# First block of a transformer kernel: norms and transposed copies in quarters over four PSUM banks, x tile 2 loaded ahead of the second V weights, and tile 3's norm moved up in the program

The kernel runs on one core of a Trainium2 chip. The metric is its device time in microseconds (us), the median of several runs. Runs of one and the same kernel lie up to 1.8 us apart (696.97 to 698.73).

In what follows TensorE (PE in the profile, PEld for its weight loads) multiplies and transposes, VectorE (DVE) computes norms, ScalarE (ACT) takes square roots and copies results out of PSUM, the memory that TensorE writes into; the Sync queue (SPq) issues transfers (DMA). A line of a profile gives start and length in us, then engine, line of the kernel, operation, what is written and read, and the number of instructions.

## The reference

A block of a transformer on 2048 rows of 1024 columns: layernorm, Q, K and V projections, attention in a window of 256, output projection, residual, then a second layernorm and a SiLU feed-forward layer.

```python
x = A_x
h = x + _A_ref(_layernorm(x, axis=-1), A_wqkv, A_wo)     # _A_ref: x @ wqkv, windowed softmax, @ wo
h2 = h + _B_ref(_layernorm(h, axis=-1), B_w1, B_w2)      # silu(x @ w1) @ w2
```

Only the first 512 rows' layernorm and V projection matter here: four tiles of 128 rows, normed on VectorE, transposed, and multiplied with the V weights in two column halves.

## The kernel before

Loads, in the order of the Sync queue (x tile 1 goes over ScalarE's queue):

```python
    load_x(0, 0)
    load_wqkv(2 * D)              # V weights 1
    load_x(0, 1, nc.scalar)
    load_wqkv(2 * D + 512)        # V weights 2
    load_x(0, 2)
    load_x(0, 3)
    load_wqkv(0)
```

Norm of one tile (statistics and norm on VectorE, square root on ScalarE) and its transposition by TensorE, with the copy out of PSUM on ScalarE:

```python
    def ln_first(xt, st, rs, j, half_done=None, ahead=None):
        ln_stats(xt, st, j, half_done)
        nc.scalar.activation(out=rs[:, j:j + 1], in_=st[:, j, 1:2], func=ACT.Sqrt, bias=eps[:], scale=1.0)
        if ahead is not None:
            ln_half(ahead[0], ahead[1], 0)
        nc.vector.reciprocal(out=rs[:, j:j + 1], in_=rs[:, j:j + 1])
        for h in range(2):
            ln_norm(xt[:, h * 512:(h + 1) * 512], st, rs, j)

    def turn_first(xt, dst, j, halves=(0, 1)):
        for h in halves:
            for i in range(4):
                kt = h * 4 + i
                nc.tensor.transpose(out=tp_ps[h][:, i * P:(i + 1) * P], in_=xt[:, kt * P:(kt + 1) * P], identity=ident[:])
            nc.scalar.copy(out=dst[:, h * 4:(h + 1) * 4, j * P:(j + 1) * P],
                           in_=tp_ps[h][:, 0:512].rearrange("p (k q) -> p k q", q=P))
```

The program order of the first block; each engine takes its own instructions in this order:

```python
    ln_first(x_ring[0], st, rs, 0, None, (x_ring[1], half))
    turn_first(x_ring[0], lnT_b[0], 0)
    ln_first(x_ring[1], st, rs, 1, half)

    def turn_1(kt):
        if kt in (5, 7):
            turn_first(x_ring[1], lnT_b[0], 1, (kt // 2 - 2,))

    v_group(0, 0, 0, act, turn_1)      # block, tile, column half: 8 matmuls and an evacuation on ScalarE
    ln_first(x_ring[2], st, rs, 2)
    v_group(0, 1, 0, act)
    v_group(0, 0, 1, act)
    turn_first(x_ring[2], lnT_b[0], 2)
    ln_first(x_ring[3], st, rs, 3)
    ln_transpose(x_ring[3], lnT_b[0], 3)    # tile 3 is transposed by DMA
    # ... three weight loads (cut)
    v_group(0, 1, 1, act)
    v_group(0, 2, 0, act)
    v_group(0, 2, 1, act)
    nc.scalar.activation(out=dummy[:], in_=eps[:], func=ACT.Exp)
    v_group(0, 3, 0, act)
    v_group(0, 3, 1, act)
```

The softmax here doesn't subtract the row's maximum and nothing guards it: scores larger than these inputs give would overflow.

## Time and profile before

| | before |
|---|---|
| time, median of 3 runs | 697.46 us (696.97 to 698.73) |
| span of the profiled run, mean granted clock | 694.9 us, 1.0 |
| TensorE busy | 684.8 us, 99% |
| landing of x tile 0 | 3.66 us |
| first K or Q matmul (end of the stretch that changes) | 22.59 us |
| from there to the end | 672.36 us |

The span is the sum of a landing (the time at which a transfer's data have all arrived), a stretch of 18.93 us from that landing to the first K or Q matmul, and a remainder in which TensorE stops only at the very end and which the change leaves alone. The measured time is some 2 us longer than the span.

### The profile page before, as it was taken

The page shows a single profiled execution, that of the slowest core. Times are in us where ns is not written, and L with a number is a line of the kernel's source. Part 1 is how long each engine was busy: PE and PEld are TensorE (multiplying, and loading weights), DVE is VectorE, ACT ScalarE, POOL GpSimd, SP SyncE. Part 2 cuts the span into 40 slices and gives each one's busy share as a digit, 9 for nine tenths or more (in the row PEclk, how much of TensorE's full clock was granted, in tenths as well). Part 3 has the DMA queues.
Part 4 walks back from the last instruction along what each step waited for, and adds up shares of the span by engine and source line. Part 5 has one row for each costly group of instructions (what it writes and reads, how often), then busy time and mean ns, then how long its engine had stood idle before and what let it go on. Part 6 is the DMA issues. An engine that isn't in the chain of part 4 may idle for free.

```text
span 694.9 us, 12233 instructions
## 1 busy us (share of the span) xinstructions
PE 684.8 (99%) x5004; PEld 331.4 (48%) x5091; DVE 288.2 (41%) x608; ACT 257.5 (37%) x322; POOL 174.5 (25%) x391
## 2 busy tenths in 40 slices
PE   8999999999999999999999999999999999999998
PEld 3444454555555555544444444444444444444445
DVE  5257646644443448544316134333133251244111
ACT  4326667777777777621310023300033100233000
POOL 1007667777777677500000000000000000000000
PEclk9999999999999999999999999999999999999999
DMA  7742231036240778880023410023300023100010
GB/s 241 257 63 68 41 99 39 18 66 187 70 129 17 211 253 274 190 311 31 31 75 100 107 38 1 1 87 72 83 1 1 10 96 92 45 1 1 30 39 24
DMA packets 76456, 60.83 MB, mean 88 GB/s; under 512 B 50288, under 2 KB 60528, under 8 KB 76400
## 3 DMA queue, kind: packets, MB, share of 16 engines
q1 hardware_dynamic: 76256, 59.78, 29.6%
q8 instruction: 40, 0.66, 0.4%
q10 hardware_dynamic: 144, 0.26, 0.1%
q14 instruction: 16, 0.13, 0.1%
HBM read 39.85 MB, written 8.39 MB: 69 GB/s over the span
## 4 chain that ended last, share of the span: by engine, by line
PE 98%; issue 1%; DVE 0%; DMA 0%; ACT 0%
PE hacc L558 18%; PE hacc L595 17%; PE acc L249 16%; PE acc L595 10%; PE acc L558 9%; PE acc L239 8%; PE acc L268 7%; PE o_ps L340 4%; PE sc L286 3%; PE hacc L268 1%; PE o_ps L355 1%; PE sc L314 1%; DMA r_o<-in_A_x_dram 0%; DVE ln_st L170 0%; PE o_ps L217 0%
## 5 line engine op out<-in xcount | busy, mean ns | idle before, releaser
L331 POOL TENSOR_SCALAR_AFFINE_SELECT r_e<-r_e 128x256 bf16<-128x256 bf16 (+1 forms) x384 | 171.6, 477 | 116.0 <-ACT r_e L323 64.5
L294 ACT ACTIVATE r_e<-sc 128x1024 bf16<-128x1024 f32 x144 | 139.5, 1021 | 45.1 <-PE sc L286 31.0
L595 PEld LDWEIGHTS <-r_a 128*128 128x128 bf16 x952 | 90.8, 98 | 103.0
L558 PEld LDWEIGHTS <-r_w 128*128 128x128 bf16 x896 | 87.3, 98 | 104.8
L595 PE MATMUL hacc<-r_a 128*128 128x512 bf16 (+2 forms) x607 | 122.0, 360 | 0.5
L558 PE MATMUL hacc<-r_e,r_w 128*128 128x512 bf16 x450 | 100.1, 379 | 0.2
L567 ACT ACTIVATE r_n<-hacc 128x512 f32<-128x512 f32 x30 | 17.9, 597 | 178.9 <-PE hacc L558 175.5
L595 PE MATMUL acc<-r_a 128*128 128x512 bf16 x330 | 73.5, 379 | 0.3
L249 PEld LDWEIGHTS <-r_w 128*128 128x128 bf16 x512 | 46.5, 98 | 57.0 <-issue 7.0
L251 DVE CAST r_a<-acc 128x512 bf16<-128x512 f32 x56 | 38.7, 691 | 72.4 <-PE acc L249 55.8
L249 PE MATMUL acc<-r_t,r_w 128*128 128x512 bf16 x241 | 58.5, 380 | 0.8
L249 PE MATMUL acc<-r_w 128*128 128x512 bf16 x245 | 57.6, 380 | 0.6
L268 PE MATMUL acc<-r_o,r_a 128*128 128x512 bf16 x196 | 48.8, 380 | 0.6
L558 PE MATMUL acc<-r_e,r_w 128*128 128x512 bf16 x207 | 48.4, 379 | 0.6
L340 PEld LDWEIGHTS <-r_e 128*128 128x128 bf16 x1152 | 39.5, 96 | 17.0
L323 ACT ACTIVATE r_e<-sc 128x1024 bf16<-128x1024 f32 x36 | 34.9, 1021 | 21.2 <-PE sc L314 20.1
L340 PE MATMUL o_ps<-r_a,r_e 128*128 128x33 bf16 x1152 | 40.2, 178 | 0.0
L610 DVE SCALAR_TENSOR_TENSOR r_t<-hacc,r_t 128x512 bf16<-128x512 f32 (+2 forms) x22 | 14.0, 635 | 56.7 <-PE hacc L595 56.7
L268 PEld LDWEIGHTS <-r_a 128*128 128x128 bf16 x256 | 23.1, 98 | 29.6 <-issue 5.1
L610 DVE SCALAR_TENSOR_TENSOR r_t<-acc,r_t 128x512 bf16<-128x512 f32 x12 | 8.3, 692 | 64.2 <-PE acc L595 58.8
L568 DVE SCALAR_TENSOR_TENSOR r_a<-r_n,hacc 128x512 bf16<-128x512 f32 x30 | 20.6, 688 | 33.0 <-ACT r_n L567 33.0
L558 PE MATMUL hacc<-r_a,r_w 128*128 128x512 bf16 x138 | 32.4, 379 | 0.3
(71 smaller groups left out, 473.4 us busy)
## 6 DMA issues: line engine op xcount, KB each, us to landing
r_w<-in_B_w_dram SPq DMA_DIRECT2D x8, 896.0 KB, 5.1
r_a<-in_B_w_dram SPq DMA_DIRECT2D x7, 1024.0 KB, 7.8
r_w<-in_A_wqkv_dram SPq DMA_DIRECT2D x6, 1024.0 KB, 8.5
h_dram<-r_t SPq DMA_DIRECT2D x16, 256.0 KB, 2.8
r_t<-h_dram SPq DMA_DIRECT2D x16, 256.0 KB, 2.8
out_dram<-r_t SPq DMA_DIRECT2D x31, 128.0 KB, 1.7
r_o<-in_A_x_dram SPq DMA_DIRECT2D x15, 256.0 KB, 4.1
r_e<-h_dram SPq DMA_DIRECT2D x3, 1024.0 KB, 5.6
```

The costliest lines, as they stand in the source:

```text
L239: nc.tensor.matmul(acc, lhsT=lnT_b[b % 2][:, kt, j * P:(j + 1) * P], rhs=wv[:, kt, c * 512:(c + 1) * 512], start=(kt == 0), stop=(kt == KT ...
L249: nc.tensor.matmul(acc, lhsT=wqk[:, kt, col0:col0 + P], rhs=lnT_b[b % 2][:, kt, :], start=(kt == 0), stop=(kt == KT - 1))
L251: copy(out=(qT, kT)[which][b][:, g, :], in_=acc)
L268: nc.tensor.matmul(acc, lhsT=qT[b][:, g, j * P:(j + 1) * P], rhs=wo[:, g, c * 512:(c + 1) * 512], start=(g == 0), stop=(g == G - 1))
L286: nc.tensor.matmul(sc[hh // 2][:, hh % 2, ch * P:(ch + nq) * P], lhsT=kT[t // 4][r0:r0 + DH, g, (t % 4) * P:(t % 4 + 1) * P], rhs=qT[b][r0 ...
L294: nc.scalar.activation(out=e, in_=sc[pair], func=ACT.Exp, scale=scale)
L323: nc.scalar.activation(out=e, in_=sc[pair], func=ACT.Exp, scale=scale)
L331: nc.gpsimd.affine_select(out=ap, in_=ap, pattern=[[0, 2], [0, n], [sgn, P]], compare_op=ALU.is_ge if upper else ALU.is_gt, fill=0.0, base ...
L340: nc.tensor.matmul(o_ps[pair][:, qt * 2 + hh, 0:VW], lhsT=e_of(i, kind, pair)[:, hh, ch * P:(ch + 1) * P], rhs=v[:, b * 4 + kt, g * 4 + pa ...
L558: nc.tensor.matmul(acc, lhsT=w1[:, kt, ft * P:(ft + 1) * P], rhs=ln2T[b][:, kt, :], start=(kt == 0), stop=(kt == KT - 1))
L595: nc.tensor.matmul(acc[:, 0:c1 - c0], lhsT=gT[:, ft, j * P:(j + 1) * P], rhs=w2[ft // 4][:, ft % 4, c0:c1], start=(ft == 0), stop=(ft == F ...
L610: nc.vector.scalar_tensor_tensor(out=t_out[j % 2][:, c0:c1], in0=acc[:, 0:c1 - c0], scalar=0.5, in1=t_in[j % 2][:, c0:c1], op0=ALU.mult, o ...
```

## The change

The intent, as far as the code tells it: norm, transpose and copy tiles in finer pieces, so that the first V matmuls start sooner; give the pieces four PSUM banks of their own (borrowed from the scores, which need them later); and have x tile 2 early enough that tile 3 is ready when TensorE wants it.

```diff
-    ps_sc = tc.tile_pool(name="ps_sc", bufs=1, ...)          # score banks: opened after the first block now
-    sc = [sc_pool.tile([P, 2, 512], F32, name=f"sc{i}") for i in range(2)]
+    ps_tp = tc.tile_pool(name="ps_tp", bufs=1, ...)
+    tp_ps = [tp_pool.tile([P, 1024], BF16, name=f"tp{i}") for i in range(4)]
-    tp_ps = [t[:].rearrange("p a b -> p (a b)").bitcast(BF16) for t in o_ps]
@@ loads
     load_x(0, 1, nc.scalar)
+    load_x(0, 2)
     load_wqkv(2 * D + 512)
-    load_x(0, 2)
     load_x(0, 3)
@@ ln_first
-        for h in range(2):
-            ln_norm(xt[:, h * 512:(h + 1) * 512], st, rs, j)
+        for h in range(4):
+            ln_norm(xt[:, h * 256:(h + 1) * 256], st, rs, j)
@@ turn_first: four pairs of transposes and copies of 128x256 in place of two of 128x512
@@ program order
-        if kt in (5, 7):
-            turn_first(x_ring[1], lnT_b[0], 1, (kt // 2 - 2,))
+        if kt == 7:
+            turn_first(x_ring[1], lnT_b[0], 1)
     v_group(0, 1, 0, act)
-    v_group(0, 0, 1, act)
-    turn_first(x_ring[2], lnT_b[0], 2)
     ln_first(x_ring[3], st, rs, 3)
     ln_transpose(x_ring[3], lnT_b[0], 3)
     # ... three weight loads (cut)
+    v_group(0, 0, 1, act)
+    turn_first(x_ring[2], lnT_b[0], 2)
     v_group(0, 1, 1, act)
```

(The first lines are abridged; warm-up matmuls, which run before the data are there and now write to other banks, are cut.) There are four main parts: quarters, banks, order of loads, and place of tile 3's norm in the program. A fifth goes with the quarters: tile 1's eight transposes now all stand before the last matmul of the first V group (k = 7), where four stood before k = 5 and four before k = 7.

More of the change, by code (lines that the diff above doesn't have):

```diff
@@ L91 @@
     r_n = big.tile([P, 1536], BF16, name="r_n")
-    ps_sc = tc.tile_pool(name="ps_sc", bufs=1, space=bass.MemoryType.PSUM, reuse_waits="tile")
-    sc_pool = ps_sc.__enter__()
-    sc = [sc_pool.tile([P, 2, 512], F32, name=f"sc{i}") for i in range(2)]
+    ps_tp = tc.tile_pool(name="ps_tp", bufs=1, space=bass.MemoryType.PSUM, reuse_waits="tile")
+    tp_pool = ps_tp.__enter__()
+    tp_ps = [tp_pool.tile([P, 1024], BF16, name=f"tp{i}") for i in range(4)]
     o_ps = [ps.tile([P, 8, 64], F32, name=f"o_ps{i}") for i in range(2)]
-    tp_ps = [t[:].rearrange("p a b -> p (a b)").bitcast(BF16) for t in o_ps]
     acc_ps = [ps.tile([P, 512], F32, name=f"acc{i}") for i in range(2)]
@@ L165 @@
     for i in range(11):
-        nc.tensor.matmul(sc[0][:, i % 2, :], lhsT=warm[:, 0, 0:P], rhs=warm[:, 0, :], start=True, stop=True)
+        nc.tensor.matmul(o_ps[i % 2][:].rearrange("p a b -> p (a b)"), lhsT=warm[:, 0, 0:P], rhs=warm[:, 0, :], start=True, stop=True)
     def ln_half(xt, stats, c):
@@ L209, in ln_first, with turn_first @@
         nc.vector.reciprocal(out=rs[:, j:j + 1], in_=rs[:, j:j + 1])
-        for h in range(2):
-            ln_norm(xt[:, h * 512:(h + 1) * 512], st, rs, j)
-    def turn_first(xt, dst, j, halves=(0, 1)):
-        for h in halves:
-            for i in range(4):
-                kt = h * 4 + i
+        for h in range(4):
+            ln_norm(xt[:, h * 256:(h + 1) * 256], st, rs, j)
+    def turn_first(xt, dst, j):
+        for h in range(4):
+            for i in range(2):
+                kt = h * 2 + i
                 nc.tensor.transpose(out=tp_ps[h][:, i * P:(i + 1) * P], in_=xt[:, kt * P:(kt + 1) * P], identity=ident[:])
-            nc.scalar.copy(out=dst[:, h * 4:(h + 1) * 4, j * P:(j + 1) * P],
-                           in_=tp_ps[h][:, 0:512].rearrange("p (k q) -> p k q", q=P))
+            nc.scalar.copy(out=dst[:, h * 2:(h + 1) * 2, j * P:(j + 1) * P],
+                           in_=tp_ps[h][:, 0:256].rearrange("p (k q) -> p k q", q=P))
     def ln_tiles(tag):
@@ L412 @@
     v_group(0, 3, 1, act)
+    ps_tp.__exit__(None, None, None)
+    ps_sc = tc.tile_pool(name="ps_sc", bufs=1, space=bass.MemoryType.PSUM, reuse_waits="tile")
+    sc_pool = ps_sc.__enter__()
+    sc = [sc_pool.tile([P, 2, 512], F32, name=f"sc{i}") for i in range(2)]
     for j in range(4):
```

## The prediction

> **What bounds the kernel now.** I read the first page, then the chain that ended last inside the first 26 us (the change touches nothing later), the waits there, the starts of single instructions in the trace, and the landings of the transfers. The page first:
>
> ```profile
> span 694.9 us, 12233 instructions
> PE 684.8 (99%) x5004; PEld 331.4 (48%) x5091; DVE 288.2 (41%) x608; ACT 257.5 (37%) x322; POOL 174.5 (25%) x391
> ...
> PEclk9999999999999999999999999999999999999999
> ...
> PE 98%; issue 1%; DVE 0%; DMA 0%; ACT 0%
> ```
>
> TensorE (PE) is the bound from end to end at the full granted clock: 98% of the chain that ended last is PE. The first of the 40 slices is the only early one below 9. So a change in the first block can win only idle time of PE in the first 19 us. The chain, stretch 0 to 26 us (start, length, what):
>
> ```profile
> 0.81 2.86 DMA r_o<-in_A_x_dram
> ...
> 3.69 1.30 DVE ln_st L170 x2
> ...
> 5.87 0.42 DVE r_o L198
> ...
> 6.34 0.41 PE o_ps L217 x4
> ...
> 6.78 1.07 ACT r_w L218 x2
> 7.85 0.20 ACT rs_a L206
> ...
> 8.07 0.17 DVE rs_a L209
> ...
> 8.28 0.42 DVE r_o L198
> ...
> 8.75 0.40 PE o_ps L217 x4
> 9.14 0.43 PE acc L239 x2
> 9.57 0.22 PE o_ps L217 x4
> 9.80 3.24 PE acc L239 x15
> ```
>
> The reader should see that PE joins for good only at 8.75 us: before that the chain is x tile 0's load, its norm, the copies of its transposes on ScalarE, and then tile 1's square root (L206), which ScalarE takes only after both copies. The V matmuls from 7.42 to 8.50 are not on the chain: PE stands from 8.50 to 8.75, waiting for tile 1's first norm half. After 9.63 PE has one gap left, at the fourth tile, which is transposed by DMA:
>
> ```profile
> 16.25 1.34 SPq L202 DMA_TRANSPOSE r_w<-r_o  x1
> ...
> 19.12 3.14 PEld L239 LDWEIGHTS <-r_w 128*128 128x128 bf16 x16 [0.52 <-DMA r_w<-r_o]
> ```
>
> By the trace, that transpose landed at 19.08 and the next matmul started at 19.126, where PE could have gone on at 18.93: 0.20 us lost. The matmul start before it was 18.715, so nothing else hides there.
>
> **What the Trainium skill says.** (1) "VectorE: DVE Perf Modes", section "The TRN2 errata — SBUF-src ops pay a fixed extra latency per instruction": every small tile pays the fixed cost again; it advises tiles of at least 512 elements. The trace agrees: norms of 128x512 follow each other 0.329 us apart, of 128x1024 0.456, so 512 elements cost 0.127 and some 0.20 of each is fixed. (2) "ScalarE: Activation LUTs", section "What ACT_TABLE_LOAD costs": 186 ns + 0.833 ns per element, overlapping by about 93 ns; that gives 613 ns for 512. Here the copies took 585 to 592 ns and followed each other 0.482 apart: near, and the trace's figures are used. (3) "TensorE: Matmul & The Clock Gate", section "Back-to-back issue gap": N/2.4 + 2.5 ns, thus 216 ns at N = 512 and 55.6 at N = 128; the trace has 216 and 56. (The same section's 131 ns for sustained 512-column streams is not seen here.) (4) "DMA: Bandwidth & Descriptors", section "Queues, rings and completion order": each engine takes descriptors in ring order. The landings agree, in order of issue on the Sync queue: x0 at 3.66, V weights 1 at 7.17, V weights 2 at 9.92, x2 at 10.56, x3 at 11.19; x1, on the other queue, at 4.41.
>
> **The change part by part.** Estimates, from those durations. A norm of 128x256: 0.411 - 0.064 = 0.347 us long, 0.329 - 0.064 = 0.265 apart. A copy of two 128x128 blocks: 0.587 - 0.218 = 0.37 long (0.218 is half of the step from 585 to 1021 ns between ScalarE's 512- and 1024-element rows), 0.482 - 0.218 = 0.26 apart.
>
> *Tile 0.* Norm quarters start at 5.87, 6.14, 6.40, 6.67; the last ends at 7.02 where the second half ended at 6.61. Transposes follow 0.06 after each quarter: the first at 6.28, the last pair at 7.07 and 7.14. Copies start some 0.32 after each quarter's first transpose: 6.60, 6.87, 7.13, 7.39, so the first lands at about 6.97 instead of 7.36. But PE works in order and has the last pair of transposes in front of the V matmuls: V starts at 7.20 (V weights 1 land at 7.17) instead of 7.42. Gained there: 0.22 us. It is not on the chain.
>
> *Tile 1.* VectorE's second statistics half starts at 6.93 instead of 6.52 (four starts of 0.265 less two of 0.329: +0.40). Aggregate 0.72 later, at 7.65, done 7.86. The square root was held at 7.74 by ScalarE's copies although its input was ready at 7.46; now the copies are out of the way at 7.66 and the input is late: it starts at 7.89 (+0.15). Reciprocal 8.22, first norm quarter 8.42, last quarter starts 9.22 and ends 9.57. PE has all of k = 0 to 6 done at 7.20 + 7 x 0.216 = 8.71, transposes quarters as they come, the last pair at 9.63 and 9.69, k = 7 at 9.75, and the next group at **9.96 instead of 9.85: +0.11**. (Before, two V matmuls stood between the halves; now PE idles between quarters, which is why the earlier V start comes to nothing.)
>
> *From there* PE is continuous: 40 matmuls of 0.2158 and 8 transposes of 0.447 in all take it from 9.96 to **19.04**, the fourth tile's first matmul.
>
> *x tile 2 ahead of V weights 2.* 256 KB take 0.64 us (10.56 - 9.92), so x2 lands near 7.8 and V weights 2 near 10.56. Those are wanted at 9.96 + 8 x 0.216 = 11.69: 1.1 us spare. Tile 2's statistics need not wait until 10.58 and start when tile 1's norm is out, 9.48. With 1.32 for statistics, 0.21 aggregate, 0.57 to the norm: norm at 11.58, tile 3's statistics at 12.63 instead of 13.33, its norm at 14.73 instead of 15.49, its last quarter done at 15.87 instead of 16.22. The transpose starts at 15.90 and lands 2.83 later at 18.72: before 19.04. **The wait of 0.20 goes.** So the fourth tile starts at 19.04 instead of 19.126.
>
> *New order on ScalarE.* Tile 3's square root (14.19) now stands in front of the evacuation of V group (0,1) and tile 2's copies. That evacuation then runs 14.4 to 15.0 and the four copies start at 14.9 to 15.7, done by 16.1. PE wants that bank and the first copy at 9.96 + 24 x 0.216 + 0.45 = 15.59: first copy at about 15.3, spare 0.3 us. Hidden, but with less room than now.
>
> *Sum*: +0.11 (tile 1) - 0.20 (transpose wait) = **-0.08 us**. Banks cost nothing (the score banks are only wanted after 22 us), and from 22.6 us on the instruction order is the same. Predicted 697.46 - 0.08 = 697.4 us.
>
> **The rivals.** (a) *Quarters pay fully*: if 256-element norms follow nearer than 0.265 us, say 0.20, the square root starts 0.26 us sooner than worked out and tile 1's last quarter 0.46 sooner: 696.9. For: the first copy ends earlier in any case, and the square root is held by copies now. Against: the fixed 0.20 us per norm, seen at two sizes. (b) *ScalarE's new order bites*: tile 3's norm comes 0.3 us later than worked out, and the copies of tile 2 stop PE at 15.6: up to 0.5 us back, 697.9. For: only 0.3 us spare. Against: statistics start 1.1 us earlier than now. (c) *V weights 2 become the wait*: would need 1.1 us of delay beyond the 0.64; 698 at most. The transfers run at a steady 370 to 400 GB/s here, so little speaks for it. (d) *The gaps between PE's quarters drop its clock*: at half rate matmuls would cost 0.43 apiece until it recovers, a few us. Against: it was fed as thinly between 6.34 and 7.42 and stayed full.
>
> **Range and chances.** All the idle time that the first block can lose after 6.34 us is under 1.1 us, 0.16% of the time, so 2% (14 us) is out of reach either way short of (d). The three runs of before spread from 696.97 to 698.73, which is more than any of the rivals (a) to (c); the range is that noise: 696.5 to 698.3. Faster by over 2% 0.005, within 0.99, slower 0.005.
>
> **What would show each step.** Norm quarters 0.26 to 0.27 apart; V matmuls from 7.2; tile 1's square root near 7.9 and free of a wait on copies; the second tile's first V matmul at 9.9 to 10.0; no matmul gap over 0.05 us from there on; V weights 2 landed by 10.7; the transpose issued near 15.9; the first K or Q matmul (now 22.590) at 22.5. Wrong if that last start is off from 22.5 by more than 0.3 us, or if the times after it differ by more than noise.

## The result

697.23 us before and 696.88 us after (medians of 6 runs each; 696.97 to 698.73 and 696.49 to 698.25). The ratio is 0.9995 with a 95% interval from 0.9982 to 1.0008: the same, within 2%.

The page of the changed kernel, its first lines:

```profile
span 695.5 us, 12334 instructions
PE 690.1 (99%) x5091; PEld 331.6 (48%) x5091; DVE 289.5 (42%) x616; ACT 257.9 (37%) x328; POOL 174.5 (25%) x391
```

This profiled span is 0.5 us *longer* than that of before, in a kernel whose median is lower. (PE busy rose by 5 us because the trace of before lacks 87 matmul records, x5004 against x5091: two later traces of the changed kernel, also with x5004, show 685.2 and 685.6.) The chain that ended last, stretch 0 to 26 us, says why (start, length, what):

```profile
0.81 3.51 DMA r_o<-in_A_x_dram
...
4.33 1.30 DVE ln_st L169 x2
...
6.52 0.36 DVE r_o L197
...
6.93 1.06 PE tp L216 x8
7.98 1.51 PE acc L238 x7
9.49 1.01 PE tp L216 x8
10.51 3.67 PE acc L238 x17
14.18 0.45 PE tp L216 x8
14.62 8.63 PE acc L238 x40
```

The first piece, x tile 0's load, took 3.51 us against 2.86, and everything behind it is shifted. By the trace 14 of its 16 arrivals were in by 3.62 us, as before; the last two came at 4.20 and 4.31. So all starts are compared from this landing from here on. After tile 0's norm, the chain shows TensorE alone where before it went through ScalarE's copies and tile 1's square root. That is in part an appearance: a transpose's record is 219 to 230 ns long and covers a short wait for the next one. Tile 1's eight transposes take 1.01 us, tile 2's, in an unbroken run, 0.45: TensorE waits there for tile 1's norm quarters one by one. The last piece, 40 matmuls in 8.63 us, is unbroken: 0.2158 each. The wait for the DMA transpose is gone. The Sync queue and VectorE, changed kernel:

```profile
16.42 1.34 SPq L201 DMA_TRANSPOSE r_w<-r_o  x1
```

```profile
9.05 1.12 DVE L197 TENSOR_SCALAR r_o<-r_o,st_a,rs_a 128x256 bf16<-128x256 bf16 x4
10.08 1.28 DVE L169 BATCH_NORM_STATS2 ln_st<-r_o 128x6 f32<-128x512 bf16 x2
```

Four norm quarters of tile 1 take 1.12 us from first start to last end (two halves took 0.74), and tile 2's statistics follow at once, where VectorE used to sit from 9.01 to 10.58 waiting for x tile 2.

| from the landing of x tile 0, us | before | after | predicted after |
|---|---|---|---|
| first V matmul | 3.75 | 3.51 | 3.54 |
| tile 1's square root | 4.07 | 4.21 | 4.23 |
| first V matmul of the second tile | 6.19 | 6.25 | 6.30 |
| DMA transpose issued | 12.59 | 12.11 | 12.24 |
| gap at the fourth tile | 0.20 | none | none |
| first K or Q matmul | 18.93 | 18.78 | 18.84 |
| from there to the end | 672.36 | 672.39 | equal |

(The predicted column is the prediction's absolute time less 3.66.) The first block is 0.14 us shorter.

### The profile page after: what moved, and what is told of

Same layout as the page of the kernel before. It is cut to its first block, busy times and chain, and to the rows that moved or that the text cites. A ratio compares the mean times of both kernels' runs of the same rounds, so it can differ in the third digit from the quotient of the medians.

```text
span 695.5 us, 12334 instructions
## 1 busy us (share of the span) xinstructions
PE 690.1 (99%) x5091; PEld 331.6 (48%) x5091; DVE 289.5 (42%) x616; ACT 257.9 (37%) x328; POOL 174.5 (25%) x391
## 4 chain that ended last, share of the span: by engine, by line
PE 99%; DMA 1%; DVE 0%; issue 0%
PE hacc L563 19%; PE hacc L600 17%; PE acc L248 16%; PE acc L600 10%; PE acc L563 9%; PE acc L238 8%; PE acc L267 7%; PE o_ps L339 4%; PE sc L285 3%; PE hacc L267 1%; PE o_ps L354 1%; PE sc L313 1%; DMA r_o<-in_A_x_dram 1%; PE tp L216 0%; DVE ln_st L169 0%; DVE r_o L197 0%
## 5 line engine op out<-in xcount | busy, mean ns | idle before, releaser
L248 PE MATMUL acc<-r_t,r_w 128*128 128x512 bf16 x256 | 60.0, 379 | 0.0
```

Source lines behind the costliest of these rows:

```text
L248: nc.tensor.matmul(acc, lhsT=wqk[:, kt, col0:col0 + P], rhs=lnT_b[b % 2][:, kt, :], start=(kt == 0), stop=(kt == KT - 1))
```

## The experiments

"The measure" is the start of the first K or Q matmul less the landing of x tile 0. All twelve kernels gave right results. Those run once are of unknown state (some executions can be slower, at a lower granted clock, and one run cannot tell); their granted clock was 1.0, and I use their traces, not their times.

**e1, order of loads alone.** The edit, on the kernel before:

```diff
     load_x(0, 1, nc.scalar)
+    load_x(0, 2)
     load_wqkv(2 * D + 512)
-    load_x(0, 2)
```

> The kernel before with x tile 2 ahead of the second V weights and nothing else. All numbers are counted from the landing of x tile 0 (3.66 us in the kernel before, 4.31 in the changed one), because that landing moves from run to run; the measure is the start of the first K or Q matmul less that landing: 18.93 before, 18.78 in the changed kernel. Theory of the prediction (the earlier tile 2 by itself takes the wait for the DMA transpose away): 18.73, no matmul gap at the fourth tile. Rival (tile 3's square root stands on ScalarE behind the copies of tile 2, so the place of tile 3's norm in the program decides): the square root stays at 11.3 after the landing, the transpose is issued at 12.6 after it as before, and the measure stays 18.93, with the gap of 0.2 us. On x tile 0 itself: if the new order of loads makes it land later, it lands near 4.3 here and in the other two kernels with this order; if it is chance, anywhere from 3.6 to 4.4.

Measured: tile 2's statistics start at 5.47 instead of 6.92, yet the transpose is issued at 12.80, the gap at the fourth tile stays, and the measure is 19.12. ScalarE of this kernel (start, length, and in brackets the idle time before):

```profile
13.85 0.59 ACT L241 CAST r_a<-acc 128x512 bf16<-128x512 f32 x1 [1.14 <-PE acc L239]
14.33 1.08 ACT L218 COPY r_w<-o_ps 128x512 bf16<-128x512 bf16 x2
15.29 0.32 ACT L206 ACTIVATE rs_a<-st_a,eps 128x1 f32<-128x1 f32 x1
```

Tile 3's square root (L206) had its input at 13.85, when VectorE's aggregate ended, and started at 15.29 behind an evacuation and two copies. The rival holds: where the square root stands in the program decides. The measure is 0.2 above the expected 18.93, and that has its own cause: TensorE was still cold when tile 0's transposes came. (I call it cold while matmuls of 128x512 start 0.427 us apart, as the warm-up matmuls do at first, and warm when they start 0.216 apart.) They came 0.106 us apart instead of 0.056, so the first V matmul came at 3.96 instead of 3.75.

**e5, place of tile 3's norm alone.** On the kernel before, only the move in the program order:

```diff
-    v_group(0, 0, 1, act)
-    turn_first(x_ring[2], lnT_b[0], 2)
     ln_first(x_ring[3], st, rs, 3)
     ln_transpose(x_ring[3], lnT_b[0], 3)
     # ... three weight loads
+    v_group(0, 0, 1, act)
+    turn_first(x_ring[2], lnT_b[0], 2)
```

> The kernel before with tile 3's norm and transpose ahead of V group (0,1) in the program, loads in the old order: the other half of what took the wait away in e2. If both are needed (tile 3's square root is held by ScalarE's copies of tile 2 in the old place, and by tile 2's late landing in the old order of loads), the DMA transpose is issued within 0.1 us of 12.6 after the landing of x tile 0, a gap of 0.1 to 0.2 us stays at the fourth tile and the measure is 18.85 to 18.93. If the place alone decides, the transpose is issued near 11.2 to 11.8, no gap, measure 18.73. In each reading up to 0.2 us more if the transposes of tile 0 run at the cold spacing of 0.106 us, as they did in e1 and in part in e2.

Measured: 19.46, worse than either expectation. The fourth tile no longer waits, but the third does. ScalarE and TensorE:

```profile
14.90 0.29 ACT L206 ACTIVATE rs_a<-st_a,eps 128x1 f32<-128x1 f32 x1 [1.97 <-DVE st_a L178]
15.10 0.57 ACT L241 CAST r_a<-acc 128x512 bf16<-128x512 f32 x1
...
15.56 1.07 ACT L218 COPY r_w<-o_ps 128x512 bf16<-128x512 bf16 x2
...
16.21 3.63 PE L239 MATMUL acc<-r_w 128*128 128x512 bf16 x16 [0.48 <-ACT r_w L218]
```

ScalarE idles 1.97 us at the square root, for x tile 2 and with it all of VectorE's work came late; evacuation and copies pile up behind it, and TensorE's matmuls stop: by the trace 0.86 us between two starts, 0.64 over the normal 0.216. This is the prediction's rival (b), real where tile 2 comes late. Sum: 18.93 + 0.08 (the transposes of tile 0 partly cold) + 0.64 - 0.20 = 19.45.

**e2 and e11, both orders, all in halves.** Both edits above together; e11 is the same kernel, timed.

> The kernel before with x tile 2 ahead and with tile 3's norm and transpose ahead of V group (0,1) in the program; norms and copies stay in halves. Both theories: the wait at the fourth tile goes, measure 18.73 (18.93 less 0.20), that is 0.05 less than in the changed kernel, if the quarters cost what the prediction says (0.11 before the second tile, with nothing won for it). If the quarters are a gain, the measure here is above 18.78.

> e2 once more, timed: norms and copies in halves, the two orders as changed. Measure 18.71 when the clock is warm at tile 0's transposes (18.79 in e2, where the first ones were cold); 0.2 us below the kernel before, level with the changed kernel within 0.2 us.

Measured: measure 18.79 in e2 (the first transposes cold: second tile at 6.26) and 18.72 in e11 (warm: 6.18). The transpose is issued at 11.24 and 11.16, no gap. So each order alone wins nothing or loses, and both together win the 0.2 us: 18.72 against 18.93 and 18.89 (e9). The changed kernel's 18.78 is 0.06 above e11: with the orders given, the quarters cost 0.06. e11's time: 696.67 us, ratio 0.9994 (0.9982 to 1.0007).

**e3, quarters and banks alone.** The changed kernel with the two orders of before.

> The changed kernel with the old order of loads and the old place of tile 3's norm: quarters and four banks alone. If the longer row of norms sits on the path (0.26 us per 256 columns): second tile's first V matmul 0.05 to 0.11 later than before from the landing of x tile 0, tile 3's norm 0.7 later, the DMA transpose issued near 13.3 after the landing instead of 12.6, a wait of 0.7 at the fourth tile, measure 19.67. If the quarters pay: measure at or below 18.93. x tile 0 lands near 3.66 if the order of loads decides it.

Measured: second tile at 6.24, transpose issued at 13.14, and TensorE:

```profile
20.12 3.63 PE L238 MATMUL acc<-r_w 128*128 128x512 bf16 x16 [0.51 <-DMA r_w<-r_o]
```

The fourth tile waits for the transpose: 0.89 us between two starts, so 0.67 lost, and the measure is 19.46. The direction and the place are as the theory has them, the size is 0.2 less. Quarters without the two orders are a loss of 0.5 us in this trace. x tile 0 landed at 4.13 with the *old* order of loads.

**e4 and e12, quarters for the copies, halves for the norms.** On the changed kernel:

```diff
-        for h in range(4):
-            ln_norm(xt[:, h * 256:(h + 1) * 256], st, rs, j)
+        for h in range(2):
+            ln_norm(xt[:, h * 512:(h + 1) * 512], st, rs, j)
```

> The changed kernel with the norms in halves again; transposed copies stay in quarters over four banks, orders as changed. If the number of norm instructions is what the quarters cost: the second statistics of tile 1 start 0.39 sooner, its first V matmuls after tile 0 stay at 3.5 after the landing of x tile 0, the second tile's first V matmul starts at 5.8 after the landing (6.25 in the changed kernel, 6.19 before), no wait after it, measure 18.36. If the copies, not the norms, are the cost: measure stays at 18.78 or more. Time 0.4 us below the changed kernel at best, which one look cannot show.

> e4 once more, timed, as the version that by its trace beats both. Measure 18.43; 0.5 us below the kernel before and 0.35 below the changed kernel, if x tile 0 lands alike; lowest median of the four.

The chain of e4, stretch 0 to 26 us:

```profile
6.26 0.30 PE tp L216 x2
...
6.58 0.66 ACT r_w L217 x2
7.24 1.66 PE acc L238 x7
8.89 0.50 PE tp L216 x8
9.39 3.27 PE acc L238 x15
```

Measured: second tile at 5.89 and 5.86, measure 18.43 and 18.40. All eight of tile 1's transposes now run in one burst of 0.50 us (1.01 in the changed kernel), as they no longer wait for quarters one by one. So what remains of the quarters does pay, 0.3 us, and the quarter norms ate it. Against the changed kernel's 18.78 the norms' cost is 0.35 to 0.39; there the edit is the norms alone. Against e11's 18.72 the gain of the rest is 0.28 to 0.32, but that is a sum of quarter copies, four banks and the new place of tile 1's transposes; no run parts these three. e12's time: 696.57 us against 697.07 before, ratio 0.9993 (0.9980 to 1.0006); the lowest median of its call, by less than the interval.

**e6, tile 1's square root ahead of tile 0's last copy** (on e4).

```diff
-    turn_first(x_ring[0], lnT_b[0], 0)
-    ln_first(x_ring[1], st, rs, 1, half)
     # ... ln_head, the statistics and the square root, is taken out of ln_first (cut)
+    turn_first(x_ring[0], lnT_b[0], 0, lambda: ln_head(x_ring[1], st, rs, 1, half))   # before the last copy
+    ln_first(x_ring[1], st, rs, 1, head=False)
```

> e4 with tile 1's square root ahead of the last copy of tile 0 on ScalarE. Tile 1's square root starts at 3.83 after the landing of x tile 0 instead of 4.06 and its norm at 4.39 instead of 4.62. If VectorE's chain alone sets tile 1's transposes, the measure falls by 0.2 to 18.2. If the first V matmuls (held by the landing of the first V weights at 7.18, that is by the load) set them as much, nothing is won: 18.43 within 0.05.

Measured: square root at 3.91 instead of 4.06, norm 0.16 sooner, and the measure is 18.44: nothing. The V matmuls started at 3.65, when the V weights had landed at 7.27 us absolute, and they stand in front of tile 1's transposes. In e4 and e6 two chains of about equal length meet there.

**e7, the first V weights in two transfers** (on e6).

```diff
-    load_wqkv(2 * D)
+    for k in (0, 4):
+        nc.sync.dma_start(out=wv[:, k:k + 4, 0:512], in_=wqkv_v[:, k:k + 4, 2 * D:2 * D + 512])
```

> e6 with the first V weights loaded as two transfers of four k tiles. First half lands near 5.9, so V matmuls start at 3.43 after the landing of x tile 0 (3.64 in e4), tile 1's transposes at 4.94 (5.15), second tile's first V matmul at 5.68 (5.89), measure 18.22. If the split load is itself late (smaller transfers, one more issue), 18.43 or more. Time 0.7 us below the kernel before and 0.55 below the changed one, if x tile 0 lands alike; the landing's spread of 0.7 us from run to run makes an interval that excludes zero doubtful.

Measured: the first V matmul comes at 3.43 and the second tile at 5.78, but the measure is 18.72. TensorE:

```profile
8.95 2.19 PE L245 MATMUL acc<-r_w 128*128 128x512 bf16 x9
11.36 1.90 PE L245 MATMUL acc<-r_w 128*128 128x512 bf16 x7 [0.22 <-DMA r_w<-in_A_wqkv_dram]
```

The second half of V weights 1 landed at 7.81, V weights 2 at 11.31 (10.59 in e4), and TensorE lost 0.38 us to the latter; the rest of the kernel took 672.59 instead of 672.36. So the split moves the wait to V weights 2. Why the whole queue is 0.7 us later I did not settle. Time 696.57 us, ratio 0.9994 (0.9981 to 1.0008).

**e8 and e10, the changed kernel again; e9, the kernel before against itself.** No edits.

> The changed kernel once more, unaltered, for two things. Measure 18.78 within 0.03 (0.2 more if its clock is late to warm). Landing of x tile 0 anywhere from 3.5 to 4.4, since in e1 to e4 it was 3.80, 3.99, 4.13 and 3.58 with no relation to the order of loads; if the changed kernel has it late for a reason of its own, 4.3 again. Time within 0.5 us of the kernel before either way, ratio 0.9995 to 1.0000.

> The changed kernel a third time, beside the kernel before against itself. If the traces tell the whole difference (measure 18.78 against 18.93, the rest equal): 0.15 us below the kernel before, give or take 0.3. If the 0.5 us by which its five runs of e8 lay below the kernel before is the change's own: 0.4 to 0.6 us below again, and more than e9 is from its own twin.

> The kernel before against itself, timed: what the timing makes of no change at all. Median within 0.3 us of the other, and an interval about as wide as those of e7 and e8 (0.9980 to 1.0005). In the trace: measure 18.93 (up to 0.2 more if the clock warms late), landing of x tile 0 between 3.4 and 4.3, 672.36 us from the first K or Q matmul to the end.

| | x tile 0 landed | first V matmul | measure | time, us | before | ratio, interval |
|---|---|---|---|---|---|---|
| e8, changed | 3.43 | 4.03 | 18.92 | 696.38 | 696.92 | 0.9992 (0.9979 to 1.0004) |
| e10, changed | 3.98 | 3.50 | 18.77 | 696.64 | 697.07 | 0.9993 (0.9980 to 1.0007) |
| e9, before | 3.77 | 3.75 | 18.89 | 696.94 | 697.07 | 0.9999 (0.9987 to 1.0012) |

e10 and e9 repeat the measure to 0.04 us. In e8 x tile 0 landed early, and TensorE then waited for V weights 1, which landed at 7.42 us:

```profile
6.22 1.06 PE L216 MATMUL tp<-ident,r_o 128*128 128x128 bf16 x8
7.46 1.68 PE L238 MATMUL acc<-r_w 128*128 128x512 bf16 x7 [0.18 <-DMA r_w<-in_A_wqkv_dram]
```

The early landing helped all the same: the first K or Q matmul started at 22.34 us, against 22.75 in e10, 0.41 sooner for a landing 0.55 sooner. The wait for the weights is not what cost the other 0.14, as the seven V matmuls were done at 5.55 from the landing and TensorE still had to wait for tile 1's last norm quarter (last transposes at 6.04). That quarter was 0.14 late (5.64 instead of 5.51 in e10), and the traces lead back to the cold clock: tile 0's transposes ran 0.106 apart, ScalarE's copies of them started at 3.25 instead of 2.94, and tile 1's square root, whose input was ready at 4.17 in both, started behind them at 4.31 instead of 4.20.

The landing of x tile 0 in all 14 traces: with the old order of loads 3.66, 4.13, 3.67 and 3.77; with the new one 4.31, 3.80, 3.99, 3.58, 3.66, 3.46, 3.43, 3.98, 3.57 and 3.92. Means 3.81 and 3.77. The orders can't be told apart by it, and the same kernel shows 3.43 to 4.31; with a spread of 0.9 us it is the largest part that I found of the scatter of runs.

**What the clock shows beyond the trace.** In e8 and e10 the changed kernel's medians lay 0.54 and 0.43 us below the kernel before, more than the 0.14 of the first block. The mean spans of those runs differ by 0.50 (695.16 and 694.66) and 0.20 (695.14 and 694.94), and a mean of five landings moves by about 0.1 by itself (an estimate: the 14 landings have a standard deviation of 0.26). Besides, the time beyond the span was 1.72 and 1.71 us on average for the changed kernel and 1.86 and 1.96 for the one before; e12 had 1.97. That part lies outside the profile, and I can't say what it is. All intervals include 1.

## Why the prediction was right, and where it was not

- **The bound** held. TensorE without a stop from the first K or Q matmul: 672.34 to 672.41 us in 13 of 14 traces (e7 aside), whatever happened before.
- **Tile 0** held: first V matmul 0.25 us sooner (predicted 0.22), and it comes to nothing, for TensorE then waits at tile 1.
- **Tile 1** held in mechanism and was mis-sized. The term "+0.11" measured +0.06. The quarters follow each other at 0.255 to 0.263 us instead of 0.265, and the small differences add up over two tiles. Rival (a), 0.20, is out.
- **The wait of 0.20 goes**: it did, but the prediction put this down to x tile 2's landing. That is the step that failed as an explanation. Its sums for tile 3 start the square root at 14.19, as soon as the statistics are done; that holds only in the new place, ahead of the evacuation and tile 2's copies. e1 shows that the earlier tile alone leaves the wait where it was, and e5 that the new place alone makes a worse one. The new place of tile 3's norm, which the prediction counted only as a risk on ScalarE, is as much a cause as the load: the win needs both.
- **ScalarE's new order** is hidden, as predicted: in the changed kernel tile 2's first copy was done at 11.48 and wanted at 11.88 from the landing, 0.4 spare (0.3 predicted). e5 shows that the risk is real when tile 2 is late.
- **V weights 2** had 1.3 us spare (1.1 predicted). They landed at 11.01, not "by 10.7", and the other signs given in absolute times (V from 7.2, square root near 7.9, transpose near 15.9) came 0.5 to 0.6 late with the landing of x tile 0; from that landing they fit.
- **Rival (d), the clock.** "Stayed full" was said too easily. The granted clock was 1.0 throughout, but in 7 of 14 traces (e1, e2, e3, e5, e6, e8, e10) all 11 warm-up matmuls started some 0.427 us apart, and in e1 and e8 all or nearly all of tile 0's transposes followed 0.106 apart (most in e6, some in e2 and e5). It cost up to 0.2 us (e1). The unaltered kernels don't tell whether the change makes it likelier (the kernel before was cold to the end of its warm-up in none of 2 traces, the changed one in 2 of 3), but e1, e2 and e5, with the halves and banks of before, have it too.
- **The sum**: -0.08 predicted, -0.11 to -0.15 by the traces (two of the kernel before, 18.93 and 18.89, against two of the changed one, 18.78 and 18.77; e8, cold, had 18.92). The prediction's own test, "off from 22.5 by more than 0.3 us", failed by the letter: the profiled run has 23.09. The test was badly made, as it was tied to one landing of x tile 0; from the landing the miss is 0.06.
- **The time** proves little. The range given, 696.5 to 698.3, is the scatter of runs, and an unchanged kernel would have met it as well (697.23). That 696.88 lies in it says nothing of the mechanism; the traces do.
- A slip in what the prediction takes from the skill: N/2.4 + 2.5 gives 55.8 ns at N = 128, not 55.6. Nothing rests on it.

Where did the gain expected of finer pieces go? Into the fixed cost of twice as many norm instructions (they start 0.26 us apart for 256 columns, 0.33 for 512), 0.35 us by e4, on the one engine whose chain sets tile 1. The copies in quarters, with their banks and the new place of tile 1's transposes, were worth having; the norms in quarters were not.

## What to carry to other kernels

Split a step into finer pieces only on the engine that has time for the fixed cost of each piece: here ScalarE's copies (0.3 us won, with what came with them), not VectorE's norms (0.35 us lost). When an operation waits, look at both ends of its wait, the data it needs and the instructions ahead of it on its own engine; moving one alone may win nothing or lose. When a change is worth less than the scatter of the runs, measure from the last event that the change does not touch (here a landing) and not from the start.

## What the Trainium skill lacked or had wrong

- "VectorE: DVE Perf Modes", section "The TRN2 errata": its row 58 + FD/Accel gives 127 ns for 256 columns at four per cycle, and its own corrected fixed term of about 150 cycles gives 223 (both are estimates worked out from the page's figures). The norm of 128x256 with two per-partition scalars took 340 to 348 ns, with starts 255 to 263 apart. I found no page with the price of such scalars on VectorE. Its advice of tiles of at least 512 elements was borne out by e4.
- "TensorE: Matmul & The Clock Gate", section "Back-to-back issue gap": it gives 131 ns as sustained spacing at N = 512. The runs show 215.8 ns, which is its formula for the isolated gap (and what the same page's account of the phases of a matmul gives).
- The same page, section "Part 4: PE-mode transpose": it says that full clock does not engage for transposes, at some 275 ns. Here transposes ran 219 ns long and 56 apart where warm-up matmuls had already come to 216 ns apart, and 314 ns long and 106 apart where they had not (e8); in e6 the spacing went from 106 to 56 among tile 0's transposes themselves. Whether transposes alone would bring the change, no run shows.
- "ScalarE: Activation LUTs", section "What ACT_TABLE_LOAD costs": 399 ns by its formula for 256 elements (an estimate from the page's figures). Four copies in a row out of PSUM took 372, 378, 392 and 405 ns, each longer than the last, with starts 0.263 to 0.268 apart; the growth is on no page that I read.
- "DMA: Bandwidth & Descriptors" has no figure for how far the landing of one and the same transfer moves: 256 KB landed between 3.43 and 4.31 us in 14 traces, and in the five latest (3.92 to 4.31) the last one or two of 16 arrivals made the difference.
